# Order of the last three product chunks of a head and the expert pieces of their group, in a fused attention and expert kernel

## Chip, cores and metric

The kernel runs on one core of a Trainium2 chip. The metric is device time in microseconds for one execution; lower is better.

## What is computed

Attention with pooled queries, then a layer in which each token goes through one of eight experts.

```python
B, H, S, D = 8, 8, 1152, 64
q_pool = q.reshape(B, H, S // 2, 2, D).mean(axis=3)          # 576 queries a head
attn = softmax(q_pool @ k.transpose / sqrt(D))               # 576 x 1152 a head
x = (attn @ v).transpose(0, 2, 1, 3).reshape(B * 576, H * D) # 4608 tokens x 512
for e in range(8):
    mask = domain_id == e
    out[mask] = relu(x[mask] @ w1[e]) @ w2[e]                # 512 -> 1024 -> 512
```

## The kernel before

**Attention.** Two heads make a pair; there are 32 pairs, numbered from 0, four to a batch. The scores of a pair are computed transposed, keys on partitions, as nine chunks of 128 keys by 576 queries for each head. They are cut into 12 steps of 432 columns (`W`), both heads side by side. So 384 steps run in all; t is the running number, `s_` the step in its pair. A step is a score on TensorE (`score`, L594, into a PSUM tile `s` of which there are three), then one exponential of 128 x 864 on ScalarE (`expo`, L606, into a tile `e`, four steps to a tile). Three chunks of 576 columns are exactly four steps.

A product multiplies one chunk of exponentials with one chunk of v (`av`, L615): five matmuls into the accumulator `acc`. The pool of `acc` has one buffer, so one head of one pair at a time is summed there. Behind a head's ninth chunk `evac` reads the sums out on VectorE: a reciprocal (L628), then a multiply (L630) into `xb`, the rows of x. The first product of the next head can't start before that. The table `AVS` says in which step the chunks are issued, counted from the start of the pair whose products they are: chunks 0 to 2 of head 0 in step 9, 3 to 5 in step 11, 6 to 8 in step 13 (step 1 of the next pair), and so on for head 1 in steps 15, 17 and 19. `AVS_END` is the table of the last pair.

**Windows.** The order on every engine is the order in which the program is written. At each even t a window is issued: score t, in window 4 (from pair 2 on) the turn of the next pair's k and q (L565, 30 transposes into another tile `s`, copied out on VectorE at L570 and L575), and score t + 1. Behind it come products whose step is even, then expert pieces. Then the odd t follows, with the products of the odd steps.

**Expert pieces.** While attention runs, TensorE also works on token tiles of the experts that are already gathered (`Fill`). A tile's tokens are turned by four transposes (L779, `turn_x`, copied to `xt` by VectorE at L782). Then come three blocks of pieces: four up pieces of four matmuls (L797), four more, and eight down pieces of one matmul (L810). Up pieces 0 to 3 write one PSUM tile `px`, which VectorE reads with the relu (L802) behind the fourth; pieces 4 to 7 write the next, and the down pieces a third, copied out at L816. The pool of `px` (`xps`) has one buffer. After a block ends, the next one waits for the next window. A planner decides in the program's text how many pieces a window gets: it adds cost constants (`C_S`, `C_AV`, `C_P`, ...) against a time for the window (`SPAN`, or two `STEP`), carrying a debt.

```python
AVS = {9 + 2 * g: [(g // 3, c, ACC) for c in range(3 * (g % 3), 3 * (g % 3) + 3)] for g in range(6)}
```

After attention the remaining expert tiles run with weights on TensorE (L1048 and L1093).

Of the kernel before, what the change touches and what calls it, by code (L numbers as in the profile page):

```python
# [19 lines left out]
def kernel(  # L20
# [14 lines left out]
    E, _, F = moe_w1.shape  # L35
    NC = S // P
    NF = F // P
    ND = Dm // P
    HP = H // 2
    NPAIR = B * HP  # L40
    QP = 96
    NJ = Sp // QP
    NQ = 5
# [7 lines left out]
    SPP = NC * Sp // W  # L51
# [529 lines left out]
    NST = NPAIR * SPP  # L581
# [28 lines left out]
    def av(p, h, c, pool):  # L610
        if c == 0:
            acc[p, h] = pool[0].tile([P, 512], FP32, name=pool[1])
        for i in range(NQ):
            o = (c % 3) * Sp + QO[i]
            nc.tensor.matmul(  # L615
                acc[p, h][:, i * (D + 1) : (i + 1) * (D + 1)],
                lhsT=et[p, c // 3][:, h, o : o + P], rhs=v16[p % NV][:, c, h, 0 : D + 1],
                start=c == 0 and i == 0, stop=c == NC - 1, skip_group_check=True,
            )

    def evac(p, h):
        b, hp = divmod(p, HP)
        if b not in xb:
            xb[b] = xpool.tile([P, NQ, Dm], F16, name="xb")
        a = acc.pop((p, h))[:, 0 : NQ * (D + 1)].rearrange("p (i d) -> p i d", i=NQ)
        u = (2 * (p if p < E else p - E) + h) * NQ
        rr = (rr0 if p < E else rrs)[:, u : u + NQ]
        nc.vector.reciprocal(rr, a[:, :, D])  # L628
        o = (2 * hp + h) * D
        nc.vector.tensor_tensor(  # L630
            out=xb[b][:, :, o : o + D], in0=a[:, :, 0:D],
            in1=rr.unsqueeze(2).broadcast_to([P, NQ, D]), op=ALU.mult,
        )
# [35 lines left out]
    def flip_x(dst, e, i):  # L669
        nc.sync.dma_start_transpose(dst, xs[e, i][:, :])  # L670
# [10 lines left out]


    ACC = (apsum, "acc")
    AVS = {9 + 2 * g: [(g // 3, c, ACC) for c in range(3 * (g % 3), 3 * (g % 3) + 3)] for g in range(6)}
    AVS_END = {
        8: [(0, c, ACC) for c in range(4)],
        10: [(0, c, ACC) for c in range(4, 6)],
# [3 lines left out]
    HOLES = ((0, 6), (0, 7), (0, 8), (1, 0))  # L691
# [48 lines left out]
    later, put, done = {}, {}, {}  # L740
# [28 lines left out]
    fb = Fill()  # L769
# [106 lines left out]
    for t in range(0, NST, 2):  # L876
        p, s_ = divmod(t, SPP)
        turns = [-(p + 1)] if s_ == (8 if p < 2 else 4) and p + 1 < NPAIR else []
        windows[t] = [t, *turns, t + 1]

    debt = 0
    for t in range(NST + 4):
        p, s_ = divmod(t, SPP)
        now[0] = t
        main = t < NST
        if main and s_ == 0 and 0 < p and p + 3 < NPAIR:
            load_q(p + 3)
        if main and p == 0:
            for step, fn, x in (
                (3, load_v, 1), (5, load_k, 2), (5, load_q, 2), (7, load_v, 2), (9, load_k, 3),  # L890
                (9, load_q, 3), (10, load_v, 3),
            ):
                if s_ == step:
                    fn(x, True)
        elif main and s_ in (2, 6) and p + 3 < NPAIR:
            (load_k if s_ == 2 else load_v)(p + 3)
        work_ns, span = 0, 0
        for it in windows.get(t, ()):
            if it < 0:
                turn(-it)  # L900
                work_ns += C_T
            else:
                score(it)
                expo(it)
                work_ns += C_S
                span += STEP
        if span:
            work_ns += C_MODE
            for off in (0, SPP):
                p0 = p - off // SPP  # L910
                if 0 <= p0 < NPAIR:
                    avs = AVS_END if p0 == NPAIR - 1 else AVS
                    work_ns += C_AV * sum(len(avs.get(s_ + off + d_, ())) for d_ in (0, 1))
            span = SPAN.get(s_, span) if 1 < p < NPAIR - 1 else span
        if t == 1:
            rest_k()
        for off in (0, SPP):
            p0 = p - off // SPP
            if 0 <= p0 < NPAIR:
                avs = AVS_END if p0 == NPAIR - 1 else AVS  # L920
                for h, c, bank in avs.get(s_ + off, ()):
                    if t >= NST and (h, c) in HOLES:
                        for _ in range(2):
                            if fb.open() or fb.blocks and fb.blocks[0][4].get("t", 2 * NST) < t:
                                fb.piece()
                    av(p0, h, c, bank)
                    if c == NC - 1:
                        evac(p0, h)
                        if p0 % HP == HP - 1 and h == 1:
                            for i in range(NQ):  # L930
                                if p0 < NPAIR - 1:
                                    put[t + 1 + i] = (p0 // HP, i)
                                else:
                                    put_x(p0 // HP, i)

        if t == NST - 2 and not fb.open() and len(turned0) < len(tiles):
            x_ = tiles[len(turned0)]
            if got.get(x_["xs"], NST) + 10 <= t:
                x_["xt"] = fill.tile([P, ND, P], F16, name="xt0")
                turn_x(x_["xt"][:, :, :], *x_["xs"])  # L940
                turned0.append(x_["xs"])
                x_["t"] = t
        if t == NST + 1:
            while fb.open():
                fb.piece()
            plan_runs()
        if main and want and t >= want[0][2] and t >= last_get + 5 and not (t in later) and not mmq and not rq:
            e, i, _ = want[0]
            if len(got) < NFX or list(got)[len(got) - NFX] in turned:
                get_x(fxs, e, i)  # L950
                got[e, i] = last_get = t
                want.pop(0)

        if first and t >= got.get(first[0], NST) + 8:
            e, i = first.pop(0)
            turned.append((e, i))
            flip_x(xt[0][:, :, i * P : (i + 1) * P], e, i)
        while main and span:
            room = (180 if p > 1 and s_ in SPAN else LAG) + span - debt - work_ns
            if fb.cur is None:  # L960
                if t < fb.ready:
                    break
                x_, able = fb.turns(t), fb.able(t)
                if x_ and room >= C_X and not (able and room >= 2 * C_P):
                    x_["xt"] = fill.tile([P, ND, P], F16, name="xt0")
                    turn_x(x_["xt"][:, :, :], *x_["xs"])
                    turned0.append(x_["xs"])
                    x_["t"], fb.ready = t, t + 1
                    work_ns += C_X
                    break  # L970
                if not able:
                    break
            if room < C_P:
                break
            fb.piece()
            work_ns += C_P
        debt = max(0, debt + work_ns - span) if span else debt + work_ns
        if t == 8:
            load_dom()
        if main and p == 0:  # L980
            for step, fn, x in (
                (2, prep_v, 0), (4, prep_k, 1), (5, prep_q, 1), (10, prep_v, 1),
            ):
                if s_ == step:
                    fn(x)
        if t in (12, 16):
            (prep_k if t == 12 else prep_q)(2)
        if main and s_ == 8 and 0 < p and p + 2 < NPAIR:
            prep_q(p + 2)
        if main and s_ == 10 and 0 < p and p + 1 < NPAIR:  # L990
            prep_v(p + 1)
        if main and s_ == 11 and 0 < p and p + 2 < NPAIR:
            prep_k(p + 2)

        if t >= 12:
            room = 0 if 18 <= t < 22 else ROOM[s_]
            while rq and room > 0 and rq[0][0] <= room and not (len(mmq) > 1 and rq[0][2:]):
                cost, fn = rq.pop(0)[:2]
                room -= cost
                fn()  # L1000
            while mmq and mmq[0][0] <= t:
                id_mm(mmq.pop(0)[1])
                if not rq and not mmq:
                    id_end()
                    rq, extra = extra, []
        if t in put:
            put_x(*put.pop(t))
        for fn in later.pop(t, []):
            fn()

        if t == (NPAIR - 3) * SPP + 9:
            ldx.close()
            wlast.append(ctx.enter_context(tc.tile_pool(name="wlast", bufs=1, side="right")))
        for e, at in enumerate(WSTEP):
            if t in at:
                load_part(e, at.index(t))
# [122 lines left out]
    for k_, r in enumerate(runs):  # L1139
# [21 lines left out]
        h = stage1(wts[e][0], xt[k_], n * P, {**at, 2: part, 7: part})  # L1161
# [122 lines left out]
    with tc.If(anyx > 0):  # L1284
        bad = nc.values_load(ovi[0:1, E + 1 : E + 2], min_val=0, max_val=1)
        with tc.If(bad > 0):
            again()
            for e in range(E):
# [3 lines left out]
                for i in range(NTC):  # L1292
                    c = e * NTC + i
# [54 lines left out]
```

## Time and profile before

| | |
|---|---|
| median of 3 runs | 429.06 us (428.65 to 430.84) |
| profiled execution, first to last instruction | 436.5 us |
| busy in it: TensorE, ScalarE, VectorE | 393.5, 337.4, 229.8 us |
| exponentials | 384, 306.0 us together |
| end of attention | about 323 us |

The page gives the profiled execution's time as its span alone. Times in rows are microseconds from the start of that span. A wait in brackets is idle time of the engine just before the row, with what ended it. A group row ("x15") gives the start of the first and the time to the end of the last. Ends of matmuls overlap with the next ones' starts, so distances are best taken from start to start.

### The profile page before, as it was taken

How to read it: one execution, taken by the hardware profiler on the slowest of the kernel's cores; microseconds unless marked ns; L12 is line 12 of the kernel's file. 1: busy time of each engine (PE TensorE's matmuls, PEld its weight loads, DVE VectorE, ACT ScalarE, POOL GpSimd, SP SyncE). 2: the span in 40 equal slices, each digit the busy share in tenths (PEclk: the TensorE clock that was granted, in tenths of full speed). 3: DMA queues.
4: the chain of work that ended last, by engine and by line, in shares of the span. 5: the costliest groups of instructions: out<-in, count | busy, mean ns of one | idle time of the engine just before them, and what ended most of it. 6: DMA issues, size and time to landing. Idle time of an engine off the chain costs nothing. (4 is left out here: it accounts for less than half of the span.)

```text
span 436.5 us, 14439 instructions
## 1 busy us (share of the span) xinstructions
PE 393.5 (90%) x6230; PEld 257.5 (59%) x6230; DVE 229.8 (53%) x628; ACT 337.4 (77%) x445; POOL 185.6 (43%) x304
## 2 busy tenths in 40 slices
PE   7888888888999999999999989989977899999993
PEld 4555555555676766766676666666753565555451
DVE  4588779874565565555656555555331235223221
ACT  5999999999999999999999989999941233323220
POOL 4542233405272742271442436443427586442413
PEclk9699999999999999999999999999998999999999
DMA  8999999994999999798884879975913589998202
GB/s 214 219 234 210 221 233 229 215 221 104 216 230 246 235 222 238 175 230 173 202 191 69 187 132 212 194 179 98 175 52 106 129 158 171 213 172 186 106 25 94
DMA packets 55757, 77.66 MB, mean 178 GB/s; under 512 B 15343, under 2 KB 44432, under 8 KB 55682
## 3 DMA queue, kind: packets, MB, share of 16 engines
q0 software_dynamic: 38384, 66.93, 75.5%
q1 hardware_dynamic: 17026, 9.58, 10.7%
q8 instruction: 50, 0.82, 0.8%
q14 instruction: 25, 0.20, 0.2%
q10 hardware_dynamic: 272, 0.13, 0.1%
HBM read 95.46 MB, written 15.21 MB: 254 GB/s over the span
## 5 line engine op out<-in xcount | busy, mean ns | idle before, releaser
L606 ACT ACTIVATE e<-s 128x864 f16<-128x864 f32 x384 | 306.0, 935 | 7.1 <-PE s L594 4.7
L594 PE MATMUL s<-qz,kq 64*128 64x432 f16 (+2 forms) x1152 | 120.6, 289 | 13.8 <-ACT e L606 10.6
L615 PE MATMUL acc<-v,e 128*128 128x65 f16 x2880 | 121.2, 194 | 9.4 <-DVE xb L630 5.5
L615 PEld LDWEIGHTS <-e 128*128 128x128 f16 x2880 | 104.1, 98 | 38.2 <-DVE xb L630 17.4
L515 POOL DMA_INDIRECT out_dram<-osb,gid x40 | 42.5, 1063 | 80.2 <-DVE osb L816 36.8
L655 POOL DMA_INDIRECT xs<-x_tok,grow x40 | 42.6, 1064 | 74.9 <-DVE xs L93 16.1
L594 PEld LDWEIGHTS <-kq 64*128 64x128 f16 x1152 | 48.2, 94 | 42.8 <-issue 25.1
L114 POOL DMA_DIRECT2D vs<-in_v_dram x32 | 23.7, 741 | 61.0 <-DVE v L540 28.0
L1093 PE MATMUL op<-w2h,hT 128*128 128x512 f16 x208 | 48.3, 387 | 0.0
L1048 PE MATMUL hp<-xt,w1h 128*128 128x256 f16 (+3 forms) x320 | 43.4, 294 | 2.6 <-ACT hT L1053 2.1
L1048 PEld LDWEIGHTS <-w1h 128*128 128x128 f16 x352 | 31.8, 98 | 20.5 <-issue 3.2
L570 DVE COPY kq<-s 128x1152 f16<-128x1152 f16 x31 | 23.5, 758 | 36.1 <-PE s L565 33.7
L1055 DVE TENSOR_SCALAR hT<-hp 128x256 f16<-128x256 f32 (+2 forms) x36 | 20.1, 558 | 40.8 <-PE hp L1048 32.1
L1099 ACT COPY osb<-op 128x512 f32<-128x512 f32 x15 | 8.8, 586 | 42.0 <-PE op L1093 31.1
L1053 ACT ACTIVATE hT<-hp 128x256 f16<-128x256 f32 (+2 forms) x36 | 17.6, 492 | 30.0 <-PE hp L1048 26.8
L628 DVE RECIPROCAL cum<-acc 128x5 f32<-128x5 f32 x48 | 9.2, 192 | 49.6 <-PE acc L615 35.3
L797 PE MATMUL px<-xt,w1h 128*128 128x128 f16 x416 | 33.8, 221 | 0.0
L1093 PEld LDWEIGHTS <-hT 128*128 128x128 f16 x208 | 20.3, 100 | 22.7 <-issue 1.6
L810 PE MATMUL px<-w2h,h 128*128 128x512 f16 x104 | 32.3, 385 | 0.0
L797 PEld LDWEIGHTS <-w1h 128*128 128x128 f16 x416 | 23.4, 98 | 12.3 <-issue 12.1
L531 DVE TENSOR_TENSOR qp<-q 96x768 f16<-96x768 f32 x31 | 29.3, 946 | 1.6 <-DMA q<-in_q_dram 1.6
L123 POOL DMA_DIRECT2D k<-in_k_dram x31 | 23.3, 751 | 4.8 <-DVE vs L93 1.7
(145 smaller groups left out, 325.0 us busy)
## 6 DMA issues: line engine op xcount, KB each, us to landing
q<-in_q_dram POOLq DMA_DIRECT2D x28, 576.0 KB
vs<-in_v_dram POOLq DMA_DIRECT2D x32, 288.0 KB
k<-in_k_dram POOLq DMA_DIRECT2D x31, 288.0 KB
w1h<-in_moe_w_dram POOLq DMA_DIRECT2D x16, 512.0 KB
w2h<-in_moe_w_dram POOLq DMA_DIRECT2D x16, 512.0 KB
x_tok<-xb SPq DMA_DIRECT2D x22, 96.0 KB
q<-in_q_dram SPq DMA_DIRECT2D x3, 576.0 KB
x_tok<-xb SPq DMA_DIRECT2D x22, 64.0 KB
```

Source lines behind the costliest of these rows:

```text
L114: nc.gpsimd.dma_start(vs[:, :, :, :], v[b, h : h + 2].rearrange("h (p c) d -> p h c d", p=P))
L515: ins = nc.gpsimd.indirect_dma_start(out=dst[:, :], out_offset=bass.IndirectOffsetOnAxis(ap=ap, axis=0), in_=src, in_offset=None, **kw,)
L531: nc.vector.tensor_tensor(out=qp[0:QP, :, :, :].rearrange("p j h d -> p h j d"), in0=q2[:, :, :, 0:D], in1=q2[:, :, :, D : 2 * D], op=ALU.add,
L570: nc.vector.tensor_copy(kq[p][:, :].rearrange("p (c r k) -> p r c k", c=NC, r=2), mt[:, :, 0 : NC * 64].rearrange("p r (c k) -> p r c k", ...
L594: nc.tensor.matmul(s[:, r, o : o + n], lhsT=kq[p][lo:hi, c * P : (c + 1) * P], rhs=qz[p % 2][lo:hi, q0 : q0 + n], start=True, stop=True,)
L606: nc.scalar.activation(e_[:, :, o : o + W], st.pop(t)[:, :, 0:W], AF.Exp, bias=0.0, scale=0.0625)
L615: nc.tensor.matmul(acc[p, h][:, i * (D + 1) : (i + 1) * (D + 1)], lhsT=et[p, c // 3][:, h, o : o + P], rhs=v16[p % NV][:, c, h, 0 : D + 1] ...
L655: nc.gpsimd.indirect_dma_start(out=dst, out_offset=None, in_=x_dram[0 : 1 + nb * Sp, :], in_offset=bass.IndirectOffsetOnAxis(ap=ap, axis=0),)
L797: nc.tensor.matmul(m[:, f % 4, :], lhsT=wts[e][0][:, cc, f * P : (f + 1) * P], rhs=h0["xt"][:, cc, :], start=cc == 0, stop=cc == ND - 1,)
L810: nc.tensor.matmul(h0["o"][:, :], lhsT=h0["h"][:, f, :], rhs=wts[e][1][:, f, :], start=f == 0, stop=f == NF - 1,)
L1048: nc.tensor.matmul(hp_[:, lo : lo + n], lhsT=w1h[:, cc, f * P : (f + 1) * P], rhs=xt[:, cc, lo : lo + n], start=cc == 0, stop=cc == ND - 1,)
L1093: nc.tensor.matmul(op_[:, :], lhsT=hT[:, f, i * P : (i + 1) * P], rhs=w2h[:, f, :], start=f == 0, stop=f == NF - 1,)
```

## The change

The products of chunks 6 to 8 move within their windows. For head 1 (step 19) the table says step 18: they are issued behind the scores of window 6 of the next pair and ahead of that window's pieces, where they were behind the pieces. For head 0 (step 13) they are issued behind the first piece of window 0 of the next pair, ahead of its other pieces; where that window has no piece, the place is the old one. The planner's sums see the same counts as before. `products` is the old loop as a function, its body unchanged.

```diff
-    AVS = {9 + 2 * g: [(g // 3, c, ACC) for c in range(3 * (g % 3), 3 * (g % 3) + 3)] for g in range(6)}
+    AVS = {
+        (18 if g == 5 else 9 + 2 * g): [(g // 3, c, ACC) for c in range(3 * (g % 3), 3 * (g % 3) + 3)]
+        for g in range(6)
+    }
+    MID = 13
...
+    def products(t, main):
+        p, s_ = divmod(t, SPP)
+        for off in (0, SPP):
...
+                    av(p0, h, c, bank)
+                    if c == NC - 1:
+                        evac(p0, h)
...
+    mid = None
...
-        for off in (0, SPP):
...
+        if mid is None or mid != t:
+            products(t, main)
...
             fb.piece()
             work_ns += C_P
+            if p and s_ + SPP + 1 == MID and p < NPAIR and mid != t + 1:
+                mid = t + 1
+                products(mid, main)
```

Lines of the changed kernel behind the table are four higher (L806 is the relu, L786 the copy of the turned tile). Three places show the order.

TensorE, window 6 of pair 17, from the second score of the window on. Before:

```order
L594 MATMUL s<-qz_97,kq 128x432 [waits Activation_49]
L594 LDWEIGHTS kq
L594 MATMUL s<-qz_97,kq 128x432
L797 LDWEIGHTS w1h
L797 MATMUL px<-xt_4206,w1h 128x128
```

Now:

```order
L594 MATMUL s<-qz_97,kq 128x432 [waits Activation_49]
L594 LDWEIGHTS kq
L594 MATMUL s<-qz_97,kq 128x432
L615 LDWEIGHTS e
L615 MATMUL acc<-v_0_100,e 128x65
```

The fifteen products follow the score at once, and the four matmuls of the up piece come behind them.

VectorE, from the turn in window 4 of pair 17 to window 8. The relu (L802, L806) belongs to the up piece of window 6. Before:

```order
L575 COPY qz_96<-s 128x6x32
L93 MEMSET xs 1x1
L802 TENSOR_SCALAR h_4249<-px 128x512
L628 RECIPROCAL cum<-acc 128x5
L630 TENSOR_TENSOR xb<-acc,cum 128x5x64
L531 TENSOR_TENSOR qp_99<-q_3952 96x2x6x64
```

Now:

```order
L575 COPY qz_96<-s 128x6x32
L93 MEMSET xs 1x1
L628 RECIPROCAL cum<-acc 128x5
L630 TENSOR_TENSOR xb<-acc,cum 128x5x64
L806 TENSOR_SCALAR h_4249<-px 128x512
L531 TENSOR_TENSOR qp_99<-q_3952 96x2x6x64
```

The read-out of the accumulator (L628, L630) stood behind the relu and stands ahead of it now.

VectorE, the same stretch of pair 20, whose window 6 has the turn of a token tile. Before:

```order
L575 COPY qz_97<-s 128x6x32
L816 COPY osb_5040<-px 128x512
L782 COPY xt_5069<-px 128x512
L628 RECIPROCAL cum<-acc 128x5
L630 TENSOR_TENSOR xb<-acc,cum 128x5x64
L93 MEMSET xs 1x1
```

Now:

```order
L575 COPY qz_97<-s 128x6x32
L820 COPY osb_5040<-px 128x512
L628 RECIPROCAL cum<-acc 128x5
L630 TENSOR_TENSOR xb<-acc,cum 128x5x64
L786 COPY xt_5086<-px 128x512
L93 MEMSET xs 1x1
```

Here the copy of the turned tile (L782, now L786) has changed places with the read-out.

## Rows read from the trace of the kernel before

**Rows 1.** Busy time by stretch: start and length, then busy us (instructions) of PE, PEld, DVE, ACT, POOL
```profile
100.00:320.00 220.00, 209.38 (x4021) 146.06 (x4021) 121.42 (x291) 214.07 (x269) 96.14 (x143) 1.00 0.89 183
```
**Rows 2.** The page, costliest groups: the exponentials
```profile
L606 ACT ACTIVATE e<-s 128x864 f16<-128x864 f32 x384 | 306.0, 935 | 7.1 <-PE s L594 4.7
```
**Rows 3.** Waits of ScalarE from 100 to 320: us, times, longest
```profile
ACT e L606 <- PE s L594: 3.8, 16, 0.4
```
**Rows 4.** Waits of TensorE from 100 to 320: us, times, longest
```profile
PE s L594 <- ACT e L606: 2.2, 11, 0.4
PE acc L615 <- DVE xb L630: 1.8, 6, 0.5
PE acc L615 <- DVE xs L93: 1.6, 4, 0.7
```
**Rows 5.** Timeline of TensorE in pair 14 (start, length, what, [idle before])
```profile
145.37 0.36 PE L594 MATMUL s<-qz,kq 64*128 64x144 f16 x4 [0.16 <-ACT e L606]
...
146.67 0.63 PE L594 MATMUL s<-qz,kq 64*128 64x288 f16 x6
...
147.46 0.61 PE L615 MATMUL acc<-v,e 128*128 128x65 f16 x15
```
**Rows 6.** Timeline of ScalarE in pair 14
```profile
147.07 2.46 ACT L606 ACTIVATE e<-s 128x864 f16<-128x864 f32 x3 [0.18 <-PE s L594]
```
**Rows 7.** Timeline of TensorE in pair 17, windows 6 to 10
```profile
176.22 0.71 PE L594 MATMUL s<-qz,kq 64*128 64x144 f16 x4
176.87 0.40 PE L797 MATMUL px<-xt,w1h 128*128 128x128 f16 x4
...
178.12 0.84 PE L797 MATMUL px<-xt,w1h 128*128 128x128 f16 x12
178.80 0.62 PE L615 MATMUL acc<-v,e 128*128 128x65 f16 x15
179.35 0.54 PE L594 MATMUL s<-qz,kq 64*128 64x288 f16 x6
```
**Rows 8.** Timeline of VectorE in pair 14
```profile
148.11 0.19 DVE L628 RECIPROCAL cum<-acc 128x5 f32<-128x5 f32 x1 [1.67 <-PE acc L615]
```
**Rows 9.** Timeline of VectorE in pair 17
```profile
177.30 0.69 DVE L802 TENSOR_SCALAR h<-px 128x512 f16<-128x512 f32 x1 [0.88 <-PE px L797]
177.91 0.18 DVE L628 RECIPROCAL cum<-acc 128x5 f32<-128x5 f32 x1
178.13 0.49 DVE L630 TENSOR_TENSOR xb<-acc,cum 128x320 f16<-128x320 f32 x1
178.53 0.94 DVE L531 TENSOR_TENSOR qp<-q 96x768 f16<-96x768 f32 x1
```
**Rows 10.** Timeline of ScalarE in pair 17
```profile
175.64 5.00 ACT L606 ACTIVATE e<-s 128x864 f16<-128x864 f32 x6
```
**Rows 11.** Timeline of ScalarE in pair 29
```profile
293.55 1.81 ACT L606 ACTIVATE e<-s 128x864 f16<-128x864 f32 x2 [0.22 <-ACT e L606]
295.77 0.89 ACT L606 ACTIVATE e<-s 128x864 f16<-128x864 f32 x1 [0.41 <-PE s L594]
```
**Rows 12.** Timeline of TensorE in pair 20, windows 6 to 8
```profile
204.91 0.86 PE L594 MATMUL s<-qz,kq 64*128 64x288 f16 x6
...
206.95 0.84 PE L797 MATMUL px<-xt,w1h 128*128 128x128 f16 x12
208.06 0.63 PE L615 MATMUL acc<-v,e 128*128 128x65 f16 x15 [0.26 <-DVE xs L93]
```
**Rows 13.** Timeline of VectorE in pair 20
```profile
206.13 0.43 DVE L782 COPY xt<-px 128x512 f16<-128x512 f16 x1 [0.49 <-PE px L779]
```
**Rows 14.** Timeline of TensorE in pair 25, windows 6 to 8
```profile
253.68 0.85 PE L594 MATMUL s<-qz,kq 64*128 64x288 f16 x6
...
255.91 0.84 PE L797 MATMUL px<-xt,w1h 128*128 128x128 f16 x12
```
**Rows 15.** Timeline of TensorE in pair 31, window 8
```profile
317.17 0.78 PE L615 MATMUL acc<-v,e 128*128 128x65 f16 x20 [0.34 <-DVE xb L630]
```

More of the change, by code (lines that the diff above doesn't have):

```diff
@@ L879 @@
         windows[t] = [t, *turns, t + 1]
+    def products(t, main):
+        p, s_ = divmod(t, SPP)
+        for off in (0, SPP):
+            p0 = p - off // SPP
+            if 0 <= p0 < NPAIR:
+                avs = AVS_END if p0 == NPAIR - 1 else AVS
+                for h, c, bank in avs.get(s_ + off, ()):
+                    if t >= NST and (h, c) in HOLES:
+                        for _ in range(2):
+                            if fb.open() or fb.blocks and fb.blocks[0][4].get("t", 2 * NST) < t:
+                                fb.piece()
+                    av(p0, h, c, bank)
+                    if c == NC - 1:
+                        evac(p0, h)
+                        if p0 % HP == HP - 1 and h == 1:
+                            for i in range(NQ):
+                                if p0 < NPAIR - 1:
+                                    put[t + 1 + i] = (p0 // HP, i)
+                                else:
+                                    put_x(p0 // HP, i)
+    mid = None
     debt = 0
@@ L916 @@
             rest_k()
-        for off in (0, SPP):
[L918 to L934, printed above, removed]
+        if mid is None or mid != t:
+            products(t, main)
         if t == NST - 2 and not fb.open() and len(turned0) < len(tiles):
```

## The prediction

> **What bounds the kernel now.** I read the stretches first. Between 100 and 320 us, pairs 11 to 31, ScalarE is busy 214.07 of 220 us and TensorE 209.38, at a granted clock of 1.00 (2.4 GHz) [rows 1]. Nothing else is near that. The exponentials are the pace: 384 of them fill 306.0 us, 0.80 us each [rows 2]. TensorE must deliver two scores, fifteen or thirty products and some expert pieces in every window of two exponentials, and it has about 5% to spare. So each hold of ScalarE in this stretch is end time, and a hold of TensorE is end time only if it arrives at ScalarE.
>
> Next, the waits of that stretch. ScalarE's largest wait is for scores: 3.8 us in 16 places [rows 3]. TensorE waits 2.2 us for exponentials before scores, and 1.8 and 1.6 us at products [rows 4]. Those two stand at the first chunk of a head. There is one accumulator bank, and the next head starts when VectorE has read the last one out. (The releaser named in the second is a one-element memset just behind such a read-out; I count it to the read-out.) The change goes at these waits.
>
> Then I took the timeline of single pairs to see which wait arrives. In pair 14 a score of window 4 starts with a wait for ScalarE [rows 5] (at 145.37): TensorE was early there, although a product earlier had been held for the accumulator. That hold cost nothing. After 145.37 the chain is score, pieces, products, score at 146.67, and ScalarE starts 0.40 later, at 147.07, having waited [rows 5, 6]. The change doesn't touch window 4, so this commonest loss stays.
>
> **The change, part by part.** Durations are from the profiled execution. Its span is 436.5 us, 7.4 above the median of the three runs shown (429.06); I carry differences over one to one.
>
> *Count of work.* Planner costs don't change, so pieces, scores and products are the same in number, and every window keeps its own. Only the order inside windows 0 and 6 of a pair moves, and with it the read-out on VectorE. On SP the writes of x come one step sooner after each batch, in the same order, and the gathers that read them are placed by step and don't move; I cost them at nothing. POOL's instructions keep their order. In pairs 1 to 9 no pieces run; there the read-out only passes small VectorE work of the routing. I cost that at nothing: TensorE's slack covers it, and without that cover the price would be one such operation a pair.
>
> *Window 6, relu case.* In pairs 12, 17, 22 and 27 (one of five: the tile pattern repeats) the piece of window 6 is the fourth up piece. Its relu frees the px bank, of which there is one, and the first matmul of window 8's pieces waits for that. Before, VectorE did relu, then read-out. Now read-out comes first, and it can't start until the products end. Pair 17, step by step:
> - The products take the piece's start, 176.87 [rows 7].
> - Products to reciprocal is 0.65 (147.46 to 148.11 [rows 5, 8]; nothing was in its way there): 177.52.
> - Reciprocal to multiply 0.22, multiply to next operation 0.40 (177.91, 178.13, 178.53 [rows 9]): the relu starts at 178.14, not 177.30.
> - The relu takes 0.69, and TensorE follows 0.13 after its end (177.30 + 0.69 = 177.99, then 178.12 [rows 7, 9]): up pieces at 178.96 instead of 178.12, so **0.84 late**.
>
> Queued behind that matmul on TensorE are the rest of twelve matmuls, fifteen products and the scores of steps 10 and 11. The six exponentials from 175.64 end at 180.64 [rows 10]; with 0.89 for one [rows 11] the last starts at 179.75, 0.40 behind its score's start at 179.35 [rows 7]. That is the same 0.40 as where ScalarE was waiting, so there is no slack: all 0.84 arrives. Four pairs make 3.4 us. Bounds per pair: 0.6, if a hold at the products of window 8 goes away in exchange (0.26 is the nearest such row [rows 12]), and 0.9.
>
> The Trainium skill, page "VectorE: DVE Perf Modes", section "The DRAIN you can't avoid", says that the next VectorE operation holds until the pipe has emptied. The row has 0.40 after a multiply of 0.49, an overlap; with the whole 0.49 in eight places the sum below would be 0.7 us higher.
>
> *Window 6, transpose case.* In pairs 15, 20, 25 and 30 the window has a turn of a token tile instead, whose VectorE copy now stands behind the read-out, and whose copy is what window 8's pieces multiply. Pair 20: the scores' group ends at 205.77 [rows 12] and the next work may start about 0.06 before such an end (176.93 against 176.87 [rows 7]), so products at 205.71; +0.65 +0.22 +0.40 gives the copy at 206.98; the copy takes 0.43 [rows 13], +0.13: pieces at 207.54 instead of 206.95. Pieces to products is 0.68 (178.12 to 178.80 [rows 7]): 208.22 against 208.06, where a wait for the accumulator now goes. Late by 0.16. Pair 25 had no such wait: scores' end 254.53 gives products at 254.47 and pieces at 256.30, against 255.91 [rows 14]: 0.39. Two of each: 1.1 us. Bounds per pair: 0 and 0.6.
>
> *Window 6, other pairs.* A piece without VectorE work follows the products. The accumulator is free 0.2 to 0.7 earlier for window 8. The waits there now don't reach ScalarE, as in pair 14, so: nothing.
>
> *Window 0.* The first piece hides the last exponential's latency, as the last of the three chunks needs step 11. The read-out moves 0.2 to 0.5 us earlier and the products of window 2 stop waiting, in about a dozen pairs. It is a gain only where the wait reached ScalarE. Pair 29 shows that: ScalarE idle 0.22 before 293.55, and up to 0.41 more at 295.77 that may hang on it [rows 11]; I take 0.3. In the last pair the wait of 0.34 [rows 15], from window 6, goes: 0.3. Others: 0.1. Gain 0.7; bounds 0.2 and 2.5 (the latter two thirds of ScalarE's 3.8).
>
> **Sum.** 3.4 + 1.1 - 0.7 = 3.8 us: 429.06 becomes **432.9 us** (the profiled span about 440.3). With the ends: 4 x 0.6 + 0 - 2.5 = -0.1, and 4 x 0.9 + 4 x 0.6 - 0.2 = 5.8, so 429.0 to 434.9.
>
> **The rivals.** About 0.5%, 2.15 us, is what a measurement of this kernel can tell from no change.
>
> *No change.* The freed accumulator pays for the late relus. The gain is at its upper bound, 2.5, and the loss half of mine in the transposes: 3.4 + 0.6 - 2.5 = 1.5 us, 430.6. For it: I haven't traced each of ScalarE's 16 waits for scores [rows 3] to its cause, and some may go with the old order. Against: most losses follow window 4. It decides from a gain of 2.4 us on.
>
> *Faster.* The wait for the accumulator is the bound; it goes in windows 2 and 8, and the new relu waits are covered because TensorE is early when it gets there. Price: 1.8 + 1.6 [rows 4], 3.4 us: 425.7. The Trainium skill, page "Perfetto Trace Analysis", section "Optimization Strategy", speaks for it: find what the most used engine's gaps wait for and make that start sooner. Here this change does so, and by that rule it gains. The trace agrees that the gaps are there, but 145.37 [rows 5] shows one given back to ScalarE. It decides if TensorE reaches window 8's pieces at least 0.84 us ahead of need; the 0.40 in pair 17 says that it doesn't.
>
> *Slower still.* Behind only one piece, the last chunk waits for the exponential of step 11 in 16 window 0s. At 0.2 each (2.2 us in 11 waits [rows 4]) that is 3.2 us of TensorE, of which perhaps a third arrives: 434.0. It decides where the first piece ends less than about 0.7 us before that exponential does.
>
> **Chances.** Mine 0.52, slower still 0.10, no change 0.30, faster 0.08. Slower by over 0.5% is the first two: 0.62; within 0.30; faster 0.08. The range: my own, 429.0 to 434.9, lowered to 428.3 to take in most of no change with the runs' spread (428.65 to 430.84): **428.3 to 435.0**. Below it lies faster; above it some of slower still.
>
> **What would show it.** Relu and token copy behind the read-out in window 6; the first up matmuls of window 8 0.8 us later in pairs 12, 17, 22 and 27, with a new ScalarE gap of that size before step 10. Waits of products for the accumulator nearly gone. Step 6's gap unchanged. I am wrong if those up matmuls start on time, if ScalarE shows no gap at step 10, or if its waits for scores fall below 3.8 us.

## The result, and the profile after

| | before | after |
|---|---|---|
| median of 4 runs, us | 429.75 (428.65 to 430.84) | 434.55 (433.44 to 436.85) |
| ratio, 95% interval | | 1.0115 (1.0067 to 1.0163) |

The change costs 4.8 us; I had forecast 3.8. A second measurement in another set of runs gave 435.08 against 430.1, ratio 1.0113 (1.0051 to 1.0175). Ratios leave out the few slow runs and need not be the quotient of the two medians.

One caution on the traces. The profiled execution of after spans 431.4 us and ran 433.44, so a span leaves out about 2.0 us, and the first trace of before, with its 436.5, is of an execution some 9 us longer than its runs' median. It holds stops of TensorE, waits that no order explains (last section), that a second trace of the same kernel mostly lacks (first experiment). So I compare after with that second trace as well as with the rows ahead of the prediction.

ScalarE's busy time from 100 to 320 us first, then its waits and TensorE's in that stretch (us, times, longest):

```profile
100.00:320.00 220.00, 208.81 (x4038) 145.48 (x4036) 120.72 (x292) 213.58 (x270) 96.49 (x143) 1.00 0.89 183
```

```profile
ACT e L606 <- PE s L594: 6.4, 17, 0.7
```

```profile
PE s L594 <- ACT e L606: 3.3, 19, 0.2
PE px L801 <- DVE h L806: 2.8, 4, 0.7
PE px L801 <- DVE xs L93: 1.3, 3, 0.4
PE px L801 <- DVE xt L786: 0.4, 1, 0.4
PE acc L615 <- DVE xb L630: 0.3, 1, 0.3
```

ScalarE's wait for scores was 3.8 us [rows 3] and is 6.4. TensorE's waits for the accumulator, 1.8 and 1.6 [rows 4], are down to 0.3: the change does what it is built to do. In their place stand 2.8 us in four waits for the relu and 1.7 in four for the token copy. (The three put to `xs L93` are the copy as well; the memset stands just behind it.) None of these stands in that view of before.

Pair 17 in the changed kernel, TensorE, windows 6 to 10 (compare [rows 7]):

```profile
177.25 0.85 PE L594 MATMUL s<-qz,kq 64*128 64x288 f16 x6
178.03 0.63 PE L615 MATMUL acc<-v,e 128*128 128x65 f16 x15
178.49 0.39 PE L801 MATMUL px<-xt,w1h 128*128 128x128 f16 x4
178.81 0.54 PE L594 MATMUL s<-qz,kq 64*128 64x432 f16 x6
180.06 0.83 PE L801 MATMUL px<-xt,w1h 128*128 128x128 f16 x12 [0.71 <-DVE h L806]
...
181.28 0.54 PE L594 MATMUL s<-qz,kq 64*128 64x288 f16 x6
```

VectorE there (compare [rows 9]):

```profile
178.69 0.20 DVE L628 RECIPROCAL cum<-acc 128x5 f32<-128x5 f32 x1 [1.47 <-PE acc L615]
178.92 0.49 DVE L630 TENSOR_TENSOR xb<-acc,cum 128x320 f16<-128x320 f32 x1
179.33 0.68 DVE L806 TENSOR_SCALAR h<-px 128x512 f16<-128x512 f32 x1
```

ScalarE there (compare [rows 10]):

```profile
176.68 4.26 ACT L606 ACTIVATE e<-s 128x864 f16<-128x864 f32 x5
181.68 0.89 ACT L606 ACTIVATE e<-s 128x864 f16<-128x864 f32 x1 [0.74 <-PE s L594]
```

In the first trace of before, the scores of window 8 that stand between the first two parts of [rows 7] are

```profile
177.65 0.54 PE L594 MATMUL s<-qz,kq 64*128 64x432 f16 x6
```

The chain is the forecast one. VectorE is idle for 1.47 us, until the products are done; reads the accumulator; and only then does the relu, at 179.33, though the piece's matmuls had started at 178.49. The up matmuls come 1.25 us behind the start of the scores of window 8 (178.81 to 180.06) where it was 0.47 in before (177.65 to 178.12). Step 10's score is late by the difference, and ScalarE has a wait of 0.74 us where its six exponentials had run without one.

### The profile page after: what moved, and what is told of

It is laid out like the page before. It is cut to its first block, busy times and chain, and to the rows that moved or that the text cites. A ratio compares the mean times of both kernels' runs of the same rounds, so it can differ in the third digit from the quotient of the medians.

```text
span 431.4 us, 14440 instructions
## 1 busy us (share of the span) xinstructions
PE 389.9 (90%) x6230; PEld 256.8 (60%) x6230; DVE 228.3 (53%) x628; ACT 336.6 (78%) x445; POOL 186.0 (43%) x304
## 5 line engine op out<-in xcount | busy, mean ns | idle before, releaser
L594 PEld LDWEIGHTS <-kq 64*128 64x128 f16 x1152 | 49.3, 94 | 50.6 <-issue 32.5
L515 POOL DMA_INDIRECT out_dram<-osb,gid x40 | 43.7, 1092 | 77.0 <-DVE osb L820 38.5
L655 POOL DMA_INDIRECT xs<-x_tok,grow x40 | 41.4, 1035 | 70.1 <-PE s L594 15.8
L1105 PE MATMUL op<-w2h,hT 128*128 128x512 f16 x208 | 47.0, 379 | 0.0
L1060 PEld LDWEIGHTS <-w1h 128*128 128x128 f16 x352 | 31.9, 98 | 17.3 <-issue 1.0
L801 PE MATMUL px<-xt,w1h 128*128 128x128 f16 x416 | 34.9, 220 | 4.6 <-DVE h L806 2.8
L814 PE MATMUL px<-w2h,h 128*128 128x512 f16 x104 | 33.5, 384 | 0.0
L628 DVE RECIPROCAL cum<-acc 128x5 f32<-128x5 f32 x48 | 9.2, 192 | 45.3 <-PE acc L615 45.1
L801 PEld LDWEIGHTS <-w1h 128*128 128x128 f16 x416 | 24.2, 97 | 14.7 <-issue 14.7
L806 DVE TENSOR_SCALAR h<-px 128x512 f16<-128x512 f32 x26 | 17.9, 690 | 17.6 <-PE px L801 17.6
```

Source lines behind the costliest of these rows:

```text
L515: ins = nc.gpsimd.indirect_dma_start(out=dst[:, :], out_offset=bass.IndirectOffsetOnAxis(ap=ap, axis=0), in_=src, in_offset=None, **kw,)
L594: nc.tensor.matmul(s[:, r, o : o + n], lhsT=kq[p][lo:hi, c * P : (c + 1) * P], rhs=qz[p % 2][lo:hi, q0 : q0 + n], start=True, stop=True,)
L655: nc.gpsimd.indirect_dma_start(out=dst, out_offset=None, in_=x_dram[0 : 1 + nb * Sp, :], in_offset=bass.IndirectOffsetOnAxis(ap=ap, axis=0),)
L801: nc.tensor.matmul(m[:, f % 4, :], lhsT=wts[e][0][:, cc, f * P : (f + 1) * P], rhs=h0["xt"][:, cc, :], start=cc == 0, stop=cc == ND - 1,)
L814: nc.tensor.matmul(h0["o"][:, :], lhsT=h0["h"][:, f, :], rhs=wts[e][1][:, f, :], start=f == 0, stop=f == NF - 1,)
L1060: nc.tensor.matmul(hp_[:, lo : lo + n], lhsT=w1h[:, cc, f * P : (f + 1) * P], rhs=xt[:, cc, lo : lo + n], start=cc == 0, stop=cc == ND - 1,)
```

## The experiments

Medians are compared within a set only: between sets the kernel before alone moved from 430.0 to 437.18 us.

**The kernel before, traced again.**

> The kernel before, unchanged, profiled once more. Theory (late readers of px): its first trace had stops of TensorE that belong to that one execution, not to the order; a second one spans about 427 us, has ScalarE waiting under 0.2 us before step 10 in all, and no wait over 0.3 us before step 8. Rival (the stops belong to the old order and the change removed them): the span is again near 436 us, with waits of 0.4 us before step 8 in pairs 15 and 20.

One run at 430.64 us, span 428.6. ScalarE's waits from 100 to 320:

```profile
ACT e L606 <- PE s L594: 2.6, 10, 0.6
```

The theory holds in part: the span is 8 us shorter, and the waits before step 8 of pairs 15 and 20 are gone. The stops in attention aren't all of the 8 us, though. From the start of the first exponential to that of the last the two traces take 311.8 and 307.6 us; behind it they go on for 117.0 and 113.5, and I hadn't looked there. Two waits of 0.57 and 0.64 us stand in other pairs, the second before step 10, so "under 0.2 us before step 10" was missed. Without these two the wait for scores is 1.4 us. Pair 20 also loses what I had put against the token copy:

```profile
205.59 0.54 PE L594 MATMUL s<-qz,kq 64*128 64x432 f16 x6
206.07 0.84 PE L797 MATMUL px<-xt,w1h 128*128 128x128 f16 x12
206.75 0.62 PE L615 MATMUL acc<-v,e 128*128 128x65 f16 x15
```

No wait for the accumulator here, where [rows 12] had 0.26. That wait came from the stop ahead of it.

**The two halves.** Head 1 alone:

```diff
-    MID = 13
+    MID = -1
```

> Head 1's half of the change alone: chunks 6 to 8 ahead of the pieces of window 6, head 0's as before. Theory: the loss is all here; slower than before by 4 to 6 us (ratio 1.010 to 1.014), ScalarE waits 0.74 us before step 10 in pairs 12, 17, 22, 27 and 0.47 us in pairs 15, 20, 25, 30, as in the changed kernel. Rival (products behind one piece wait for the last exponential): about half or less of the loss, under 2 us.

Head 0 alone:

```diff
-        (18 if g == 5 else 9 + 2 * g): [...]
+        9 + 2 * g: [...]
```

> Head 0's half alone: chunks 6 to 8 behind the first piece of window 0, head 1's as before. Theory: within 1 us of before (ratio 0.998 to 1.002); the products of window 2 no longer wait for the accumulator, and that arrives nowhere. Rival (they wait for the exponential of step 11): 2 to 3 us slower, with TensorE waiting for ScalarE at the products of window 0. Rival (the accumulator bounds): 1.5 us or more faster.

Head 1: 435.39 against 430.0, ratio 1.0108 (1.0048 to 1.0168). Its TensorE has the four relu waits of the changed kernel, to the tenth:

```profile
PE px L801 <- DVE h L806: 2.8, 4, 0.7
```

Head 0: 429.58 against 430.0, ratio 0.9992 (0.9959 to 1.0025). ScalarE's waits, from 100 to 320:

```profile
ACT e L606 <- PE s L594: 1.6, 9, 0.2
```

So the loss is in head 1's half. Head 0's half is worth nothing that can be measured, and the rival of the last exponential falls: no such loss shows.

**The old place in eight windows.**

```diff
+    AVS_OLD = {(19 if s == 18 else s): x for s, x in AVS.items()}
+    LATE = (12, 15, 17, 20, 22, 25, 27, 30)
...
-                avs = AVS_END if p0 == NPAIR - 1 else AVS
+                avs = AVS_END if p0 == NPAIR - 1 else AVS_OLD if p0 + 1 in LATE else AVS
```

> The change, but with the old place of head 1's chunks (step 19) in pairs 12, 15, 17, 20, 22, 25, 27 and 30, whose window 6 holds a relu or a token copy. Theory: all of the 4.8 us of waits before step 10 goes; within 1 us of before (ratio 0.997 to 1.003), and 4 to 5 us faster than the changed kernel. Rival (the loss comes from the order in the other pairs too): still 1.5 us or more slower than before.

429.94 against 430.0, ratio 0.9995 (0.9957 to 1.0032). ScalarE, from 100 to 320:

```profile
ACT e L606 <- PE s L594: 1.6, 9, 0.2
```

6.4 less 1.6 is 4.8 us in eight waits, and the measured loss is 4.8 us. Only eight of the 31 windows 6 are different from the changed kernel, and without them no loss can be measured. That the two figures agree to the tenth is in part chance, as the sum by terms shows below: a wait in pair 6 isn't among the eight, and the part behind attention differs too.

**Relu and token copy apart.** The same edit with four pairs each: `LATE = (15, 20, 25, 30)` leaves the relu case early, `LATE = (12, 17, 22, 27)` the copy.

> The change, with the old place only in pairs 15, 20, 25 and 30 (token copy in window 6). Theory: four waits of 0.74 us before step 10, 2.9 us; with 0.5 us of pair 6 about 3 us slower than before (ratio 1.005 to 1.009). Rival (the eight waits aren't what the time hangs on): as the changed kernel, or as before.

> The change, with the old place only in pairs 12, 17, 22 and 27 (relu in window 6). Theory: four waits of 0.47 us before step 10, 1.9 us; with 0.5 us of pair 6 about 2 us slower than before (ratio 1.002 to 1.007). Rival (only the relu costs, and the copy's delay is paid back by the accumulator's wait): within 0.5 us of before.

Relu alone: 439.76 against 437.18, ratio 1.0061 (1.0026 to 1.0096). Copy alone: 440.79, ratio 1.0064 (1.0028 to 1.01). Each is slower than before and about half of the whole. That the relu costs more is in the traces of the changed kernel (0.74 a pair against 0.47) but not in these times, whose intervals overlap; this set's traces also have stops of TensorE. The rival that only the relu costs falls.

**TensorE's order without VectorE's.** Head 1's read-out is held until the pieces of the window are issued:

```diff
+                        if main and s_ + off == 18:
+                            held.append((p0, h))
+                        else:
+                            read_out(p0, h, t)
...
+        while held:
+            read_out(*held.pop(0), t)
         debt = max(0, debt + work_ns - span) if span else debt + work_ns
```

> The change, but head 1's read-out is issued on VectorE behind the pieces of window 6: TensorE's order is the changed kernel's, VectorE's is that of before. Theory: the relu or copy is late for two reasons, its matmuls come one group of products later on TensorE, and it stands behind the read-out on VectorE. From the rows, products to relu was 0.65 + 0.22 + 0.40 = 1.27 us with the read-out between; without it 0.59 (products to piece) + 0.43 (piece to relu) = 1.02, so 0.25 comes back in each of the eight pairs: ScalarE waits 0.49 before step 10 in pairs 12, 17, 22, 27 and 0.22 in 15, 20, 25, 30, 2.8 us in all instead of 4.8; about 3 us slower than before. Rival (the order on VectorE is all of it): no waits before step 10, within 1 us of before. Rival (TensorE's order is all of it): 4.8 us of waits as in the changed kernel.

439.81 against 437.18, ratio 1.0053 (1.001 to 1.0095). Pair 17, TensorE:

```profile
177.46 0.63 PE L615 MATMUL acc<-v,e 128*128 128x65 f16 x15
177.93 0.38 PE L801 MATMUL px<-xt,w1h 128*128 128x128 f16 x4
178.25 0.54 PE L594 MATMUL s<-qz,kq 64*128 64x432 f16 x6
179.09 0.83 PE L801 MATMUL px<-xt,w1h 128*128 128x128 f16 x12 [0.31 <-DVE h L806]
```

VectorE:

```profile
178.35 0.69 DVE L806 TENSOR_SCALAR h<-px 128x512 f16<-128x512 f32 x1 [1.34 <-PE px L801]
178.96 0.18 DVE L628 RECIPROCAL cum<-acc 128x5 f32<-128x5 f32 x1
```

ScalarE:

```profile
180.71 0.89 ACT L606 ACTIVATE e<-s 128x864 f16<-128x864 f32 x1 [0.34 <-PE s L594]
```

Products to relu is 0.89 us (177.46 to 178.35) against 1.30 with the read-out between (178.03 to 179.33). So 0.41 of the delay is VectorE's order and the rest, 0.31 of waiting here, TensorE's: the piece itself runs one group of products later. By the trace both rivals that put all on one engine fall; the time alone, 0.4 to 4.2 us by its interval, would not exclude one within 1 us of before. My figure for the wait was 0.15 too high: a piece starts 0.47 behind the products, and I had taken 0.59. In the copy's pairs 25 and 30 ScalarE waits 0.07 and 0.13 (0.22 expected); pairs 15 and 20 have a stop beside it and 0.32.

**What is left: step 6.** In both kernels TensorE waits in window 4 for a score tile, and ScalarE then waits before step 6. Chunks of head 1 can fill that wait. On the kernel before:

```diff
             if it < 0:
                 turn(-it)
                 work_ns += C_T
+                if p >= FROM:
+                    for c in (3, 4):
+                        av(p - 1, 1, c, ACC)
...
                 for h, c, bank in avs.get(s_ + off, ()):
+                    if s_ + off == 17 and c < 5 and FROM <= p < NPAIR - 1 and off:
+                        continue
```

> Not a part of the change: the kernel before, with two of head 1's chunks (3 and 4) moved in window 4 from behind the pieces to between the turn and the second score, from pair 11 on. TensorE waits there about 0.33 us for an exponential to free a score tile, and the score of step 6 then comes 0.1 to 0.4 us late, 5.5 us in all 20 pairs: the largest wait that is left in both kernels. Theory (that wait is filled by 0.36 us of products): step 6's waits fall by about 0.28 us each where they are that long, 3 to 4.3 us faster than before (ratio 0.990 to 0.994). Rival (the second score comes too late and step 5 waits instead): no difference, with new waits before step 5.

437.16 against 437.18, ratio 0.998 (0.9949 to 1.0011): no difference. From start to start of the exponentials, less the 0.77 us that most have, the delays ahead of step 6 fell from 5.7 us (second trace of before) to 2.2 in pairs 10 to 31, and those ahead of step 5 rose from nothing to 4.6. The rival was right: two chunks overfill the wait, and the second score now comes as late as the products make it. One chunk then (`(3,)` and `c < 4`), on the kernel before and on head 0's half:

> The kernel before, with one of head 1's chunks (3) between the turn and the second score of window 4, from pair 11 on; two had moved the wait from step 6 to step 5. Theory (the score of step 5 has 0.1 us to spare, and one chunk of 0.18 us fits into the wait of 0.33): step 6's waits fall by 0.15 to 0.2 us a pair, to about 2 us in pairs 10 to 31, with none before step 5; 2.5 to 3.5 us faster (ratio 0.992 to 0.995). Rival (that stretch is bound by TensorE's work, whatever its order): the waits move to steps 5 or 8, within 1 us of before.

> The same on head 0's half of the change. Theory: head 0's half is worth nothing by itself and stays so: the same as the kernel with one chunk alone within 1 us. Rival (with step 6's wait gone, the accumulator's wait in window 2 arrives): 1 us or more faster than that one.

Alone 429.49 against 430.1, ratio 0.9961 (0.992 to 1.0003): inconclusive, and less than I expected. In its trace the delays ahead of step 6 are still 4.6 us, and those ahead of step 8 fell from 1.3 in the second trace of before to 0.2. With head 0's half 428.48, ratio 0.9948 (0.9917 to 0.9979): faster, by about 2 us. Whether head 0's half adds to the one chunk or not, these two can't say. This version beats both kernels.

**The changed kernel again.**

> The changed kernel, unchanged, for a second measurement and trace beside the others. Theory: 4 to 6 us slower than before (ratio 1.009 to 1.014); eight waits before step 10 as in its first trace, 4.8 us together. Rival (the first measurement was of one chip): a ratio below 1.005.

Ratio 1.0113, as told above, and the same line to the tenth:

```profile
ACT e L606 <- PE s L594: 6.4, 17, 0.7
```

## Why the prediction came out as it did

The direction, the mechanism and its places were right; the sum was 1.0 us short (3.8 against 4.8), inside the range. That it came so close is in part luck, since terms were off in both directions. By its terms (a delay is the time from start to start of two exponentials, less 0.77 us):

*Relu case, 0.84 a pair.* Measured 0.78 at the up matmuls (1.25 less 0.47) and 0.74 at ScalarE. Products to reciprocal took 0.66, to the multiply 0.23, to the relu 0.41, all as worked out from [rows 5, 8, 9]. What was off is the last step: TensorE follows the relu after 0.05 (180.01 to 180.06). The 0.13 that I read from [rows 7, 9] wasn't a wait for the relu; TensorE simply got there then. Four pairs: 3.0 us for my 3.4. No slack, as argued.

*Transpose case, 1.1 us.* This term was mis-sized. Pair 20 in the changed kernel, TensorE:

```profile
207.60 0.63 PE L615 MATMUL acc<-v,e 128*128 128x65 f16 x15
...
208.38 0.54 PE L594 MATMUL s<-qz,kq 64*128 64x432 f16 x6
209.37 0.83 PE L801 MATMUL px<-xt,w1h 128*128 128x128 f16 x12 [0.44 <-DVE xs L93]
```

VectorE:

```profile
208.27 0.19 DVE L628 RECIPROCAL cum<-acc 128x5 f32<-128x5 f32 x1 [0.87 <-PE acc L615]
208.49 0.49 DVE L630 TENSOR_TENSOR xb<-acc,cum 128x320 f16<-128x320 f32 x1
208.90 0.41 DVE L786 COPY xt<-px 128x512 f16<-128x512 f16 x1
```

The up matmuls start 0.99 us behind the scores, where it was 0.48 in the second trace of before (205.59 to 206.07): 0.51 late, and ScalarE waits 0.47 in each of the four pairs, so 1.9 us. In pair 20 I had taken off a wait for the accumulator that belonged to a stop of the first trace, and I had put a second pair at the same 0.16.

Pair 25 is another case. There the token turn waits for the px bank in both traces of before. In the second:

```profile
252.10 0.86 PE L594 MATMUL s<-qz,kq 64*128 64x288 f16 x6
253.09 0.38 PE L779 MATMUL px<-ident,xs 128*128 128x128 f16 x4
```

The turn starts 0.99 behind the scores, where it is 0.80 in pair 20 of the same trace (204.02 to 204.82). Head 0's half hasn't this wait (251.95 to 252.74), and neither has the changed kernel. The delays of pair 25 are 0.58 us in both traces of before, 0.40 with head 0's half and 0.90 in the changed kernel: 0.32 more than before, so the 0.39 was nearly right for this pair, but not for the one I had counted with it. In pairs 15, 20 and 30 it is 0.5 each.

*Gain, 0.7 us.* About 0.2 to 0.3 of it is there, in the last pair, where I had put 0.3 for the wait in [rows 15]. That wait stands in the second trace of before too:

```profile
312.74 0.78 PE L615 MATMUL acc<-v,e 128*128 128x65 f16 x20 [0.34 <-DVE xb L630]
```

It is in head 0's half as well, and neither trace of the changed kernel has it. The delays of pair 31 are 0.23 and 0.31 us in the two traces of before and 0.21 in head 0's half; in both traces of the changed kernel and in that of the eight old places, which all have the new order in this pair, there is none. The 0.18 of pair 25, told above, is a gain too, one that I hadn't named. Pair 29's waits [rows 11], put at 0.3, aren't in the second trace of before: another stop. Most waits for the accumulator that did go were given back to ScalarE's exponentials, as at 145.37 [rows 5]; TensorE's wait for score tiles rose to 3.3 us in 19 places, from 1.6 in 9 in the second trace of before.

*Early pairs, nothing.* Wrong by 0.5 us. In pair 6, the accumulator's wait in window 2 of the changed kernel, and what follows:

```profile
67.78 0.63 PE L615 MATMUL acc<-v,e 128*128 128x65 f16 x15 [0.77 <-DVE xb L630]
```

```profile
69.14 1.67 ACT L606 ACTIVATE e<-s 128x864 f16<-128x864 f32 x2 [0.47 <-PE s L594]
```

VectorE is full with routing there. Head 1's half has this wait, and head 0's half hasn't, so it comes with the read-out that now stands ahead of the routing operations in window 6. That those operations are then pushed into the next pair is argued from the order, not tried.

Together: 4 x 0.74 + 4 x 0.47 + 0.47 = 5.3 us of new waits at ScalarE, for 4.8 us (2.9 to 7.0 by the interval). Attention itself agrees with the 5.3: from the start of the first exponential to that of the last it takes 311.8 us in both traces of the changed kernel, 306.3 with head 0's half and 306.6 with the eight old places, so 5.2 to 5.5 more; none of these traces has a stop there. Behind it the changed kernel's traces end sooner, after 111.7 and 112.6 us, against 113.4 to 113.7 in those two and the second trace of before. No term stood for this; its cause wasn't traced.

Of the two rules of the Trainium skill that I weighed, the whole 0.49 of "The DRAIN you can't avoid" (Trainium skill, page "VectorE: DVE Perf Modes") didn't show; the relu started 0.41 behind the multiply. The rule to make what the gaps wait for start sooner (Trainium skill, page "Perfetto Trace Analysis", section "Optimization Strategy") did remove TensorE's gaps at the accumulator, 3.4 us to 0.3, and the kernel became slower: 4.5 us of waits at the one bank of px took their place, and these arrive at ScalarE.

Step 6's waits stayed, as forecast; ScalarE has a wait of 0.18 there in pair 14, before [rows 6] and after.

## What to carry to other kernels

Ahead of moving a group of instructions forward on an engine, list what it moves back, and for each of these who reads it on another engine and how many buffers it has; a reader of a tile with one buffer that ends up behind the moved group is the price. Read how much of a wait arrives at the engine that sets the pace before counting on its removal: a wait that ends ahead of another wait is free. And take two traces of the kernel before, if gains are to be read from single gaps: what only one of them has is no part of the order. What both have can be, even where it looks like an accident: the token turn's wait in pair 25 was of this kind.

## What the runs showed of the hardware

The first trace of before has, in pair 26, a wait of ScalarE that no order explains:

```profile
ACT e L606 <- PE px L797: 1.0, 1, 1.0
```

TensorE's rows go on there at their usual distances up to 260.97, but ScalarE, which waits for them, is released only at 261.82, and the next products start at 261.85. Other stops show in TensorE's own rows. In head 1's half a group of fifteen products is cut in two, with nothing named that the second part waits for; ScalarE then waits 1.84:

```profile
287.77 0.39 PE L615 MATMUL acc<-v,e 128*128 128x65 f16 x7 [1.72 <-issue]
```

Such stops hold ScalarE for 0.2 to 2.1 us and stand in most of the traces taken here; both traces of after and those of head 0's half and of the eight old places have none in that stretch. Many are at different pairs in different executions, but not all: ScalarE's waits before step 8 of pairs 15 and 20, 0.4 us each in the first trace of before, come back at 0.2 to 0.3 in all four traces of one set of runs, and no other trace has them.

That set is the one in which the kernel before took 437.18 us, against 430.0 and 430.1. It ran on another chip than the other two sets. Its traces have more stops, and behind the start of the last exponential they go on for 116.5 to 117.5 us, where the traces of the other two sets and of after take 111.7 to 113.7; the first trace of before, whose chip isn't on record, takes 117.0 there. So the 7 us lie in both parts, and a part of what looked like accidents of one execution may belong to the chip. The cause of the stops wasn't found.
